# Turning keys and queries one slot later, and queueing the P*V norm ahead of a slot's other evacuations

## The chip, the cores and the metric

One core of one Trainium2 chip. The metric is the device time of one execution in microseconds (us). An execution counts as slow when it is over 1.5% above the fastest of the same kernel, and as fast otherwise. Medians are of all executions of a kernel; ratios use the fast ones alone, and a profile that fell on a slow one is marked. TensorE (PE in the profile; PEld are its weight loads) multiplies matrices, VectorE (DVE) and ScalarE (ACT) empty its results out of PSUM, GpSimd (POOL) converts inputs, SyncE (SP) issues nearly all DMAs.

## The reference

```python
# q, k, v: (8 batches, 8 heads, 576 rows, 64), float32
scores = scale * np.matmul(q, k.transpose(0, 1, 3, 2))
thresh = np.max(scores, axis=-1, keepdims=True) - tau
scores = np.where(scores >= thresh, scores, -1000000000.0)
scores = scores - np.max(scores, axis=-1, keepdims=True)
attn = np.exp(scores)
attn = attn / (np.sum(attn, axis=-1, keepdims=True) + 1e-09)
x = np.matmul(attn, v)        # ... reordered to (8*576, 512)
h = (x @ w1) * (x @ w2) @ w3
return h @ w_out
```

## The kernel before

Two heads of a batch form a "pair" (32 pairs), a pair has nine chunks of 128 score rows, and the kernel is one software-pipelined loop over 288 "slots", one chunk each. The order in which the program calls the operations is the order in each engine's queue. Cut to what matters here:

```python
for t in range(end + 1):
    if t < total:
        scores(t)                  # TensorE: 4 matmuls into a tile S (tag "S", 3 buffers)
    if 0 < t <= total:
        maximum(t - 1)             # VectorE: row maximum and copy; frees that S
    leave()                        # evacuation of the last feed-forward product
    while later: later.pop(0)()    # SyncE: the two DMAs that make kB
    while late: late.pop(0)()      # VectorE: copies of turned keys or queries
    # ... ScalarE's masks and exponentials; DMA transposes of finished probabilities (SyncE)
    if 0 <= c < total and PATH[c % 4] == "P":
        select(c)                  # VectorE: every fourth chunk
    if t in norms:
        next(norms[t])             # VectorE: reciprocal, and x = av * reciprocal; frees av
    if t % 3 == 0 and 0 < t <= total:
        threshold(t - 1)
    # ...
    for f, a in plan.pop(t, ()):
        f(*a)                      # turns, P*V (attend), loads, casts
    # ... then feed-forward matmuls, as TensorE's clock of the plan allows
```

Three kinds of tile share the three score buffers: the scores S, the result `av` of P*V (one per pair, filled at the ends of two consecutive slots) and `tp`, in which TensorE turns the keys or queries of a later pair:

```python
def turn(n, nm):
    tp = psum.tile([128, 2048], BF16, tag="S", name="tp", bufs=3)
    for i, src in enumerate(blocks):                       # 9 transposes on TensorE
        nc.tensor.transpose(tp[:, i * 128:(i + 1) * 128], src, ident[:, :])
    def way():                                             # one slot later
        nc.vector.tensor_copy(st, tp[:, 0:2 * S])          # kT or qT; frees tp
        if nm == "k":
            def swap():                                    # one more slot later
                nc.sync.dma_start(kB[0:64, :], st[64:128, :])
                nc.sync.dma_start(kB[64:128, :], st[0:64, :])
            later.append(swap)
    late.append(way)
```

The scores need kT and kB, the keys with their two halves exchanged. A free buffer goes to the next tile in the order in which the freeing instructions are queued (pair 16 in the prediction shows it).

## Time and profile before

| | before |
|---|---|
| time, median of 3 (range) | 522.89 us (522.27 to 523.69) |
| profiled span | 520.3 us |
| steady state, slots 36 to 252 (24 pairs) | 346.8 us, 14.45 us a pair |
| TensorE busy in it | 93%, VectorE 88%, ScalarE 84% |
| feed-forward products left for the end | 54.8 us |

The steady state is where a change of order can act. TensorE leads in it, so the idle stretches in front of its instructions, by what ended them, are the quantity to follow. The lines are shown in the prediction.

### The profile page before, as it was taken

What the parts mean: (1) busy time and instruction counts of PE and PEld (TensorE: products, weight loads), DVE (VectorE), ACT (ScalarE), POOL (GpSimd) and SP (SyncE); (2) the same over time, 40 slices, a digit from 0 to 9 for tenths busy, and PEclk for the clock granted to TensorE, in tenths of its full rate; (3) what the DMA queues carried; (4) which work ended last, traced back from release to release, by engine and by line L of the source; (5) the groups of instructions that cost most, each with busy time, mean ns of one, the idle gap of its engine ahead of it and who ended that gap; (6) DMA issues with size and microseconds to landing.
All of it is one profiled execution on the core that took longest, in us unless ns stands there. A gap on an engine that the chain in (4) does not pass through costs nothing.

```text
span 520.3 us, 13159 instructions
## 1 busy us (share of the span) xinstructions
PE 471.9 (91%) x4922; PEld 327.0 (63%) x4982; DVE 421.3 (81%) x987; ACT 411.0 (79%) x711; POOL 176.9 (34%) x265
## 2 busy tenths in 40 slices
PE   4788989999999999979998999999988999999996
PEld 3566666666666666656665666666656767554674
DVE  4999988899988898969888988888999988773222
ACT  3798887888889888958898888788878998895442
POOL 6958630443318231543217330631276100000000
PEclk9999999999999999989999999999999999999999
DMA  8999627989899997998799999999999974873211
GB/s 238 197 227 194 159 66 145 182 173 189 171 209 222 196 204 165 218 196 180 152 235 217 192 221 193 204 178 205 208 200 260 214 139 97 151 137 70 82 49 73
DMA packets 203936, 91.15 MB, mean 175 GB/s; under 512 B 169696, under 2 KB 195296, under 8 KB 203872
## 3 DMA queue, kind: packets, MB, share of 16 engines
q1 hardware_dynamic: 199936, 84.54, 77.3%
q0 software_dynamic: 3392, 5.24, 6.0%
q8 instruction: 39, 0.64, 0.5%
q10 hardware_dynamic: 544, 0.52, 0.3%
q14 instruction: 25, 0.20, 0.1%
HBM read 39.32 MB, written 9.44 MB: 94 GB/s over the span
## 4 chain that ended last, share of the span: by engine, by line
PE 54%; DVE 19%; ACT 13%; issue 7%; DMA 6%; SPq 1%; DVEq 0%; ACTq 0%
PE ab L445 14%; PE S L252 13%; PE yp L460 9%; DVE sc L277 7%; ACT y L333 5%; PE av L367 4%; PE both L445 4%; DVE pm L347 3%; DMA pTm<-pms 3%; ACT pm L337 3%; PE tp L203 3%; DVE x L373 3%; PE wp L134 2%; ACT e L343 2%; PE S L258 2%
## 5 line engine op out<-in xcount | busy, mean ns | idle before, releaser
L277 DVE TENSOR_SCALAR_CACHE_REDUCE sc<-S 128x576 f32<-128x576 f32 x288 | 215.0, 751 | 29.7 <-PE S L252 19.6
L333 ACT ACTIVATE y<-sc,thr 128x576 bf16<-128x576 f32 x216 | 162.4, 769 | 11.6 <-DVE thr L285 11.5
L252 PE MATMUL S<-kT,qT 128*128 128x288 bf16 x464 | 125.1, 290 | 12.3 <-DVE x L373 8.9
L252 PE MATMUL S<-kB,qT 128*128 128x288 bf16 x464 | 124.6, 289 | 3.3 <-DMA kB<-kT 3.2
L337 ACT ACTIVATE pm<-y 128x576 bf16<-128x576 bf16 x192 | 126.5, 674 | 0.0
L252 PEld LDWEIGHTS <-qT 128*128 128x128 bf16 x928 | 84.6, 99 | 58.2 <-DVE x L373 12.7
L460 PE MATMUL yp<-wcb,ab 128*128 128x512 bf16 x269 | 67.5, 379 | 1.1 <-ACT ys L452 0.2
L430 DVE TENSOR_TENSOR ab<-ah,ab 128x512 bf16<-128x512 bf16 (+1 forms) x65 | 42.1, 648 | 26.3 <-PE ab L445 22.3
L427 ACT ACTIVATE ah<-ab 128x512 bf16<-128x512 f32 (+1 forms) x65 | 36.7, 564 | 31.0 <-PE ab L445 30.8
L347 DVE SCALAR_TENSOR_TENSOR pm<-sc,thr,e 128x576 bf16<-128x576 f32 x64 | 59.1, 923 | 0.0
L445 PE MATMUL ab<-xm,w1b 128*128 128x512 bf16 x211 | 56.6, 379 | 1.9 <-ACT xm L397 0.9
L445 PE MATMUL ab<-xm,w2b 128*128 128x512 bf16 x203 | 53.7, 379 | 2.1 <-DVE ab L430 0.6
L367 PE MATMUL av<-vb,pT 128*128 128x65 bf16 x1056 | 50.7, 194 | 1.1 <-DMA pT<-pm 1.1
L367 PEld LDWEIGHTS <-pT 128*128 128x128 bf16 x1320 | 47.9, 98 | 4.5 <-DMA pT<-pm 1.3
L445 PEld LDWEIGHTS <-w1b 128*128 128x128 bf16 x352 | 34.1, 98 | 24.4 <-issue 4.5
L343 ACT ACTIVATE e<-sc 128x576 f32<-128x576 f32 x72 | 48.4, 673 | 0.4 <-DVE sc L277 0.4
L445 PEld LDWEIGHTS <-w2b 128*128 128x128 bf16 x352 | 33.6, 98 | 21.2 <-issue 3.1
L452 ACT ACTIVATE ys<-yp 128x512 f32<-128x512 f32 x36 | 21.4, 595 | 30.0 <-PE yp L460 30.0
L460 PEld LDWEIGHTS <-ab 128*128 128x128 bf16 x288 | 27.8, 98 | 25.0 <-issue 0.3
L367 PE MATMUL av<-vz,pT 128*128 128x65 bf16 x256 | 42.6, 192 | 0.0
L161 POOL CAST khl<-kf 128x512 bf16<-128x512 f32 x31 | 20.1, 647 | 58.0 <-DMA kf<-in_k_dram 41.3
L162 POOL TENSOR_TENSOR qhl<-qf,qhl 128x512 bf16<-128x512 f32 x31 | 37.5, 1209 | 2.5
(105 smaller groups left out, 739.8 us busy)
## 6 DMA issues: line engine op xcount, KB each, us to landing
vf<-in_v_dram SPq DMA_DIRECT2D x32, 256.0 KB, 3.4
out_dram<-ys SPq DMA_DIRECT2D x16, 512.0 KB, 3.8
kB<-kT SPq DMA_DIRECT2D x56, 144.0 KB, 3.5
kf<-in_k_dram SPq DMA_DIRECT2D x31, 256.0 KB, 3.7
qf<-in_q_dram SPq DMA_DIRECT2D x31, 256.0 KB, 3.5
w<-in_moe_w_dram POOLq DMA_DIRECT2D x8, 256.0 KB, 5.2
pT<-pm SPq DMA_TRANSPOSE x112, 3.7
kt<-in_k_dram SPq DMA_DIRECT2D x16, 64.0 KB, 3.1
```

What stands on the lines that cost most here:

```text
L162: lo.tensor_tensor(hl[1], src, hl[0], ALU.subtract)
L252: nc.tensor.matmul(sp[:, half, 0:HB], lhsT=t["qT"][:, q0:q0 + 128], rhs=kk[w][:, c0:c0 + HB], start=(w == 0), stop=(w == 1))
L277: nc.vector.tensor_scalar(sc[:, :].rearrange("p (a b) -> p a b", a=2), sp[:, :, 0:HB], 1.0, -3e38, ALU.mult, ALU.max, accum_out=maxima[c / ...
L333: nc.scalar.activation(t["y"][:, :], t.pop("sc")[:, :], AF.Prelu, scale=-1.0, bias=t.pop("thr"), alpha=0.125 / CUT)
L337: nc.scalar.activation(place(*stream[c]), chunks.pop(c)["y"][:, :], AF.Exp, scale=-CUT)
L343: nc.scalar.activation(t["e"][:, :], t["sc"][:, :], AF.Exp, scale=0.125)
L347: nc.vector.scalar_tensor_tensor(out=place(*stream[c]), in0=t["sc"][:, :], scalar=t["thr"], in1=t["e"][:, :], op0=ALU.is_ge, op1=ALU.mult)
L367: nc.tensor.matmul(dst, lhsT=lhsT, rhs=rhs, start=(g == 0), stop=(g == 4))
L427: return lambda: nc.scalar.activation(ah[:, 0:nt], p[:, 0:nt], AF.Copy)
L430: return lambda: nc.vector.tensor_tensor(ab[:, 0:nt], ah[:, 0:nt], p[:, 0:nt], ALU.mult)
L445: nc.tensor.matmul(p[:, 0:nt], lhsT=w[:, c, f * 128:(f + 1) * 128], rhs=x(c), start=(c == 0), stop=(c == 3))
L460: nc.tensor.matmul(yp[0:c1 - c0, :], lhsT=abs_[f][:, c0:c1], rhs=wcb[:, f, :], start=(f == 0), stop=(f == NF - 1))
```

## The change

The norm waits behind whatever VectorE has in its queue in that slot, and TensorE's next scores wait for the norm. The change puts the norm right behind the maximum, and moves the turns so that the key transposes no longer fall into the slot of the norm.

```diff
-    turns = {n: (first[n] - 8, first[n] - 6) for n in range(2, NPAIR)}
+    turns = {n: (first[n] - 7, first[n] - 5) for n in range(2, NPAIR)}
@@
             if 0 < t <= total:
                 maximum(t - 1)
+            if t in norms:
+                next(norms[t])
             leave()
@@
                 select(c)
-            if t in norms:
-                next(norms[t])
             if t % 3 == 0 and 0 < t <= total:
```

Pairs 0 and 1 and the last batch (pairs 28 to 31) keep their turns. The plan counts the conversions on GpSimd and the loads of keys, queries, values and tail rows from the turns, so for the moved pairs these come one slot later too.

## The prediction

> **What bounds the kernel now.** I read the page's busy shares first, then the busy time by stretch, the waits, one pair of heads in order of time, and SyncE's queue. The kernel walks through 288 chunks of scores ("slots"), nine to a pair of heads. From 66.4 to 413.2 us (slots 36 to 252, so 24 pairs of 14.45 us) it is in a steady state, which this row shows; the feed-forward products that are left run alone from 465 us on.
>
> ```profile
> PE 471.9 (91%) x4922; PEld 327.0 (63%) x4982; DVE 421.3 (81%) x987; ACT 411.0 (79%) x711; POOL 176.9 (34%) x265
> ...
> core 0: us, PE busy (x) PEld busy (x) DVE busy (x) ACT busy (x) POOL busy (x), PEclk, DMA share, GB/s
> 66.40:413.20 346.80, 320.86 (x3456) 223.16 (x3499) 305.81 (x717) 291.27 (x505) 128.86 (x166) 1.00 0.94 193
> ```
>
> In the steady state TensorE is busy for 320.86/346.80 = 93%, VectorE for 88%, ScalarE for 84%: three engines close to their limit that wait for each other in turn, with TensorE in front. No instruction is worth much, but an idle stretch of TensorE is. These are TensorE's waits that the change touches, with one of VectorE's:
>
> ```profile
> engine line waited for: us in total, times, longest us
> ...
> DVE ab L430 <- PE ab L445: 22.3, 26, 5.0
> ...
> PEld L252 <- DVE x L373: 12.7, 21, 1.2
> ...
> PE S L252 <- DVE x L373: 8.9, 18, 1.0
> ...
> PEld L252 <- DMA kB<-kT: 4.3, 4, 2.1
> ...
> PE S L252 <- DMA kB<-kT: 3.2, 3, 1.9
> ```
>
> The largest steady wait of TensorE is the score matmuls' wait for the norm x (8.9 us in 18 pairs, about 0.85 us in every second pair and 0.2 to 0.33 in the others). The PEld row is the same wait seen by the weight loads, not another 12.7 us. The second wait is for kB, the copy of the keys with its halves exchanged by DMA. Here is the norm's wait in pair 16:
>
> ```profile
> start us, us, engine line op out<-in xcount [idle before <-releaser]
> ...
> 239.58 0.74 DVE L277 TENSOR_SCALAR_CACHE_REDUCE sc<-S 128x576 f32<-128x576 f32 x1
> ...
> 241.03 0.69 DVE L430 TENSOR_TENSOR ab<-ah,ab 128x512 bf16<-128x512 bf16 x1 [0.69 <-PE ab L445]
> ...
> 241.25 0.39 PE L203 MATMUL tp<-ident,khl 128*128 128x128 bf16 x4
> ...
> 241.63 0.21 DVE L371 RECIPROCAL rcp<-av 128x10 f32<-128x10 f32 x1
> ...
> 241.88 0.82 DVE L373 TENSOR_TENSOR x<-av,rcp 128x640 bf16<-128x640 f32 x1
> ...
> 242.76 0.30 PE L252 MATMUL S<-kT,qT 128*128 128x288 bf16 x1 [0.85 <-DVE x L373]
> ```
>
> What to see: P*V (av) was finished at 240.05, and VectorE's maximum of the slot with its read-out at 240.34. VectorE then sat idle for 0.69 us until TensorE had made the feed-forward product, because that evacuation stands ahead of the norm in its queue. Meanwhile the transposes of the keys (tp) took the score buffer that the maximum had just freed, so the next scores got the buffer of av, which only the norm frees, and TensorE stood for 0.85 us. It is a loop: TensorE's product, its evacuation, the norm, TensorE's scores. I call the slot in which this happens slot 1 of the nine (P*V is made at the ends of slots 8 and 0).
>
> **What the Trainium skill says.** "PSUM — Partial Sum Buffer", section "Engine vs sequencer instructions": the queues of VectorE and ScalarE are strict FIFO. The trace agrees: the norm's inputs lay ready for 1.3 us behind an instruction that itself waited. "Perfetto Trace Analysis", section "Optimization Strategy": the same gap repeating on the engine that should be saturated can mean that there is no SBUF or PSUM left for the next tile. The trace agrees: the gap is a wait for one of three score buffers. The same page, "Identifying the Most-Contended Engine", warns that matmul busy time is no measure of closeness to the limit; here the weight loads are busy for 64% of the stretch against 93% for matmuls, so TensorE can be asked for more than its 7% of idle time suggests. The same page, "DMA Instruction — HWDGE (DVE, Sync)": the issuing sequencer is free only when it has issued, and the data's movement is not in that window. The trace agrees: a kB issue takes about 0.5 us and lands 3.5 us (median) after its start.
>
> **The change, part by part.** No instruction is added, removed or resized: only order changes.
>
> *The norm first.* In slot 1 the norm (0.21 + 0.82 us) moves ahead of the feed-forward evacuation (0.65 us) and of a select (0.92 us, where there is one). By the rows above it would start at 240.34 and end near 241.4 instead of 242.70, and the evacuation, whose product is ready at about 240.9, follows with no idle time.
>
> *The turns one slot later.* The key transposes move from the end of slot 1 to the end of slot 2, the query ones from slot 3 to slot 4. Buffers are handed out in the order in which their readers are queued (pair 16 shows it). So the scores of slot 2 now get the buffer that the maximum of slot 1 frees, and the transposes get av's buffer, one block of scores later. In pair 16: the scores come at 241.3, or at 242.1 if a feed-forward step slips in before them; both are after 240.34, so nothing waits. The transposes come near 242.6, and the norm ended near 241.4: nothing waits. The scores of slot 3 need the maximum of slot 2, which VectorE reaches at 241.4 + 0.7 = 242.1 and ends at 242.9: in time. The whole wait goes, and VectorE's idle 0.69 us is used. Gain: all 18 waits, **-8.9 us**.
>
> *What lateness costs.* kT comes one slot (about 1.55 us) later, and so does its exchange kB, which the scores of the next pair need. SyncE's queue for kB of pair 17:
>
> ```profile
> 244.08 0.47 SPq L226 DMA_DIRECT2D kB<-kT  x1
> 244.60 0.59 SPq L227 DMA_DIRECT2D kB<-kT  x1
> 245.52 2.18 SPq L323 DMA_TRANSPOSE pT<-pm  x1
> 247.79 1.28 SPq L328 DMA_TRANSPOSE pTm<-pms  x1
> ```
>
> kB is queued at the start of slot 3 now, of slot 4 then. The transposed probabilities of slot 3 will stand ahead of it instead of behind: one DMA transpose in pairs n with n mod 4 = 0 or 3, two where n mod 4 = 1, none newly where n mod 4 = 2 (there it is ahead already). I took from the trace, for pairs 6 to 27, when kB landed and when its scores began. The margin is now 4.9 to 5.6 us for the pairs with n mod 4 = 1, 1.9 to 5.4 for 0, -2.1 to 5.2 for 3, -0.9 to 2.5 for 2; three pairs are below zero (15, 18, 26: the three kB waits above). Moving each issue behind those transposes at their old times costs 2.5 to 4.7 us where one is added and 4.1 to 5.0 us where two are. That leaves pairs 17 and 23 at about -0.1, 12 at -0.4, 24 at -0.9, 19 at -2.2, 15 at -4.8, and adds 6.4 us of waiting. If the transposes move up by the 1.2 us of the two kB issues that no longer precede them, wherever their inputs are ready, only pairs 15 and 19 lose more than 0.2 us: 2.6 us in all. I take **+4.5 us**. (Queries have 5.1 us or more to spare and keep 3.5.)
>
> *Small terms.* Pairs 28 to 31 keep their turns, so the queries of pair 27 and the keys of pair 28 fall into one slot, with two copies of 0.75 us: I estimate **+0.5 us**. Thresholds of slot 3 now stand behind the key copy of 0.75 us; ScalarE waits for thresholds 11.5 us in all, but has over 2 us of idle time a pair: 0.
>
> Sum: -8.9 + 4.5 + 0.5 = -3.9 us, from 522.9 to **519.0 us** (-0.7%).
>
> **The rivals.** *A: kB takes the place of the norm.* For it: margins already below zero in three pairs, a DMA share of 0.94 in the steady state, and SyncE's single queue. If the delays are the upper ones, and those pairs push the landings of later ones, the loss is 8 to 12 us and the time 522 to 526. Against it: 10 of the 22 pairs had over 3 us to spare. *B: VectorE takes over.* Its work between two maxima does not shrink, so the scores might wait one block later for the next maximum. For it: 88% busy. Against it: 41 us of idle time in the steady state (346.80 - 305.81), and the gap in slot 1 (idle 0.69 us) that the norm fills. If B held half the gain back: about 523. *C: the loop gains more than its wait.* A shorter cycle also feeds VectorE and ScalarE sooner (VectorE waits 22.3 us for the feed-forward products), and kB's issues have room: 509 to 513. Against it: with the wait gone, a pair such as 16 leaves TensorE no visible idle time at all. *D: the norm waits for P*V.* Queued so early, it may reach VectorE before av is done and block what is behind it. In pair 16 it would not (240.05 against 240.34); where VectorE follows closely it could be 0.1 to 0.3 us a pair, below VectorE's idle time.
>
> **Range and chances.** 519.0 is the sum. From 511.5 (C in part, kB without loss) to 526 (A with part of B) should hold 8 times in 10. Over 2% faster needs less than 512.4, more than the whole wait on the norm: 0.08. Over 2% slower needs 533.3, some 19 us of new waits: 0.02. Within 2%: 0.90.
>
> **What would show it right or wrong.** The rows for TensorE waiting on x should fall from 8.9 us to under 2. The feed-forward evacuation should follow the norm in slot 1 without idle time. The kB waits (3.2 us in 3) should grow to some 6 to 10 us in 4 to 8 pairs, first in pairs 15 and 19; if they stay at 3, the time falls towards 514, and if they pass 12, I was wrong about the sign. A new row of TensorE waiting for sc or for ab in the score matmuls would speak for B. The last stretch of feed-forward products (55 us) should not change. If the time moves by more than 8 us either way while x's wait goes as foreseen, the step on kB is at fault.

## The result, and the profile after

The changed kernel takes 518.09 us (median of 4, 514.77 to 518.31) against 522.96 us of the kernel before in the same rounds. The ratio is 0.9892, with a 95% interval of 0.985 to 0.9934. It is 0.9875 (0.983 to 0.9919) when measured once more below. A ratio is the mean time of one kernel's fast runs over that of the other's of the same rounds, so not quite the ratio of the medians.

The profiled execution of the changed kernel was its fastest, so its span of 513.0 us flatters it by some 3 us. First the busy shares and the steady state (columns as in the prediction's row):

```profile
PE 467.4 (91%) x4922; PEld 325.7 (63%) x4982; DVE 425.2 (83%) x987; ACT 410.4 (80%) x711; POOL 177.9 (35%) x265
...
67.00:405.50 338.50, 316.72 (x3457) 222.07 (x3500) 308.21 (x717) 290.45 (x505) 127.82 (x166) 1.00 0.97 198
```

The same 24 pairs take 338.5 us against 346.8 (14.10 us a pair against 14.45). The last stretch is the same 54.8 us. So the whole gain of this profile lies in the steady state (8.3 us, against 7.3 us of the span). The waits of TensorE in the changed kernel:

```profile
PEld L252 <- DMA kB<-kT: 10.9, 8, 3.0
PE S L252 <- DMA kB<-kT: 9.6, 8, 2.8
...
PEld L367 <- DMA pTm<-pms: 1.5, 2, 1.1
PEld L252 <- DVE x L373: 1.5, 2, 1.0
...
PE av L367 <- DMA pTm<-pms: 1.3, 2, 0.9
...
PE S L252 <- DVE x L373: 1.0, 2, 0.7
```

The wait for x went from 8.9 us in 18 places to 1.0 in 2. The wait for kB went from 3.2 us in 3 places to 9.6 in 8. P*V's wait for the DMA-transposed probabilities (pT and pTm) fell from 4.2 us (3.1 + 1.1) to 1.7 (1.3 + 0.4).

Pair 16 shows how the wait for x went. This is the same slot 1 as in the prediction's lines:

```profile
234.76 0.76 DVE L277 TENSOR_SCALAR_CACHE_REDUCE sc<-S 128x576 f32<-128x576 f32 x1 [0.30 <-ACT pm L337]
...
235.46 0.22 DVE L371 RECIPROCAL rcp<-av 128x10 f32<-128x10 f32 x1
...
235.72 0.82 DVE L373 TENSOR_TENSOR x<-av,rcp 128x640 bf16<-128x640 f32 x1
...
236.46 0.68 DVE L430 TENSOR_TENSOR ab<-ah,ab 128x512 bf16<-128x512 bf16 x1
...
237.48 0.29 PE L252 MATMUL S<-kT,qT 128*128 128x288 bf16 x1
...
237.97 0.39 PE L203 MATMUL tp<-ident,khl 128*128 128x128 bf16 x4
```

The norm follows the maximum at once, the feed-forward evacuation follows the norm with no idle time in brackets, and the scores of slot 2 and then the key transposes start with no wait. SyncE's queue for kB of pair 17, whose counterpart stands in the prediction:

```profile
240.11 1.28 SPq L323 DMA_TRANSPOSE pT<-pm  x1
241.48 1.24 SPq L328 DMA_TRANSPOSE pTm<-pms  x1
242.81 0.54 SPq L226 DMA_DIRECT2D kB<-kT  x1
243.40 0.59 SPq L227 DMA_DIRECT2D kB<-kT  x1
```

kB now stands behind two transposes. In this pair it landed 1.7 us before its scores began. Before the change it had 4.9 us to spare.

### The profile page after: what moved, and what is told of

It reads as the page before. It is cut to its first block, busy times and chain, and to the rows that moved or that the text cites.

```text
span 513.0 us, 13187 instructions
## 1 busy us (share of the span) xinstructions
PE 467.4 (91%) x4922; PEld 325.7 (63%) x4982; DVE 425.2 (83%) x987; ACT 410.4 (80%) x711; POOL 177.9 (35%) x265
## 2 busy tenths in 40 slices
DMA packets 203936, 91.15 MB, mean 178 GB/s; under 512 B 169696, under 2 KB 195296, under 8 KB 203872
## 4 chain that ended last, share of the span: by engine, by line
PE 61%; DVE 14%; DMA 8%; ACT 7%; issue 6%; POOL 3%; SPq 0%; DVEq 0%; ACTq 0%; POOLq 0%
PE S L252 15%; PE ab L445 14%; PE yp L460 10%; PE av L367 6%; DVE sc L277 6%; PE tp L203 4%; PE both L445 4%; DMA kB<-kT 3%; PE wp L134 3%; ACT y L333 2%; DVE pm L347 2%; DMA qt<-in_q_dram 2%; PE S L258 2%; DMA pTm<-pms 2%; DVE ab L430 1%
## 5 line engine op out<-in xcount | busy, mean ns | idle before, releaser
L252 PEld LDWEIGHTS <-qT 128*128 128x128 bf16 x928 | 86.0, 98 | 55.5 <-DMA kB<-kT 10.9
L347 DVE SCALAR_TENSOR_TENSOR pm<-sc,thr,e 128x576 bf16<-128x576 f32 x64 | 55.3, 864 | 0.0
L162 POOL TENSOR_TENSOR khl<-kf,khl 128x512 bf16<-128x512 f32 x31 | 36.6, 1181 | 2.5
```

What stands on the lines that cost most here:

```text
L162: lo.tensor_tensor(hl[1], src, hl[0], ALU.subtract)
L252: nc.tensor.matmul(sp[:, half, 0:HB], lhsT=t["qT"][:, q0:q0 + 128], rhs=kk[w][:, c0:c0 + HB], start=(w == 0), stop=(w == 1))
L347: nc.vector.scalar_tensor_tensor(out=place(*stream[c]), in0=t["sc"][:, :], scalar=t["thr"], in1=t["e"][:, :], op0=ALU.is_ge, op1=ALU.mult)
```

## The experiments

Twelve kernels ran, all correct except two. Every one was timed in 5 rounds against the kernel before, and one profile was taken of each. The kernels of one group ran on one chip and share the runs of the kernel before (medians 524.49, 526.82, 526.38 and 524.71 us in the four groups). Ratios are against the kernel before.

### First group: which part of the change does it?

**The changed kernel again.** No edit.

> The changed kernel once more, for common rounds and a second profile, since its profiled execution (514.8 us) was 3.3 us below its three others (518). Theory 1 (the gain is the wait on the norm minus new waits for kB): ratio 0.986 to 0.993, waits of the score matmuls on x under 2 us, on kB 8 to 11 us in about 8 places. Rival (the fast profile was the rule and part of the gain is something else): ratio under 0.985.

Ratio 0.9875 (518.87 us median, 514.59 us the fastest). In its profile x costs 1.0 us and kB 12.1 us in 7 places. 4.0 us of that is one wait for pair 1's kB at the very start, where 0.6 us stood in the first profile and 0.1 us in the kernel before. Its steady state is 338.1 us, as in the first profile. The two profiles differ by 4.9 us, and the start makes 5.3 us of it (slot 36 is reached at 72.3 us against 67.0). So the fast first profile was luck at the start, and the gain of 8 us in the steady state repeats. Part of it is lost at the start, though: by the profiles, kernels with the old turns reach slot 36 at 66.4 to 67.8 us, and those with late turns (leaving out kB on ScalarE) at 66.5 to 72.3. Half-clock stretches before slot 36 (3.4 to 6.8 us) occur only among the latter. Why the start suffers is not shown. kB's 12.1 us lie above the 8 to 11 expected; without pair 1 they are 8.1.

**The turns alone.** The norm goes back to its old place.

```diff
-            if t in norms:
-                next(norms[t])        # ahead of leave()
+            if t in norms:
+                next(norms[t])        # behind select(c), as before
```

> The turns one slot later, the norm at its old place. Theory 1: the scores of slot 2 no longer get av's buffer, so their wait on x goes also without the early norm; the key transposes now wait for the norm instead, 0.1 to 0.7 us in every second pair, 3 us in all; kB as in the changed kernel, 8 to 11 us. Ratio 0.990 to 0.999. Rival (the early norm carries the gain): the wait on x moves whole to the transposes, 8 us or more, and the ratio is 1.00 to 1.01.

Ratio 0.988 (0.9839 to 0.9921): the same as the whole change. The waits in its profile:

```profile
PE S L252 <- DMA kB<-kT: 6.3, 6, 1.8
...
PE av L367 <- DMA pTm<-pms: 1.7, 2, 1.4
...
PE tp L203 <- DVE x L373: 1.4, 2, 1.0
```

The scores' wait for x fell to 0.3 us in one place, and 1.4 us of waiting for x turned up at the key transposes instead (3 us were expected). So the later turns alone remove the wait, as they should if the scores of slot 2 take the buffer that a maximum frees. The ratio is better than the 0.990 to 0.999 expected, and kB costs 6.3 us where 8 to 11 were expected. The early norm on top of it is worth nothing that these runs can show.

**The norm alone.** The turns go back to their old slots.

```diff
-    turns = {n: (first[n] - 7, first[n] - 5) for n in range(2, NPAIR)}
+    turns = {n: (first[n] - 8, first[n] - 6) for n in range(2, NPAIR)}
```

> The norm first, the turns at their old slots: kB is as early as before. Theory 1: the norm ends near 1.8 us after the slot's maximum began, before TensorE reaches the scores of slot 2, so the wait on x falls from 8.9 to 0 to 3 us while kB waits stay at 3 to 4 us: ratio 0.980 to 0.988, faster than the changed kernel by 2 to 5 us. Rival (without the other buffer the scores still meet the norm): 4 us or more of the wait on x stay, ratio 0.990 to 1.000.

Ratio 0.9986 (0.9937 to 1.0036): nothing gained that these runs can show, against 0.980 to 0.988 expected. The theory failed here; the ratio lies where the rival put it, but not for the rival's reason, which needed 4 us or more of waiting for x. Its profile:

```profile
PE av L367 <- DMA pTm<-pms: 6.0, 4, 2.8
PEld L252 <- DVE x L373: 5.6, 13, 1.0
PE S L252 <- DMA kB<-kT: 5.2, 4, 2.8
...
PE S L252 <- DVE x L373: 3.1, 12, 0.7
```

The wait for x did fall, by 5.8 us, to within a tenth of the upper end of what was expected. But the waits for pT, pTm and kB together rose from 7.4 us to 12.4 (6.0 + 1.2 + 5.2), and TensorE's clock was halved for 6.8 us and for 3.4 us in the loop, against 3.4 us once in the kernel before. The timed executions say the same: their mean granted clock is 0.988, against 0.9935 for the kernel before in the same rounds. SyncE's queue has the same order as in the kernel before, so a new order in it is not what made these DMAs late. Why they were late is not shown. The waits for pT and pTm differ much between profiles with the old turns: 4.2 us in the kernel before, 7.2 here, and 7.6 (6.6 + 1.0) in the kernel with the old turns and pair 1's kB made on TensorE (third group).

**kB into SyncE's queue at once.** The changed kernel, but the DMAs are queued in the slot of the key copy, ahead of that slot's transposes.

```diff
-                later.append(swap)
+                swap()
```

> The changed kernel, with the exchange of the keys put into SyncE's queue in the slot of the key copy, ahead of that slot's transposes, not at the start of the next slot. Theory 1: kB is issued within 0.3 us of the end of the key copy in most pairs, its waits fall from about 9.6 to 2 to 5 us, and the kernel gains 3 to 6 us on the changed one: ratio 0.976 to 0.984. Rival (kB's lateness costs nothing on the whole, since TensorE, once ahead, would wait for something else): kB waits fall but the time stays within 1.5 us of the changed kernel's, with longer waits for transposed probabilities or maxima.

Ratio 0.9981: worse than the changed kernel by about 1%, where a gain was expected. kB was issued within 0.05 us of the end of the key copy in seven of the pairs 6 to 27 (in none of them in the changed kernel), not in most of them as expected, and its waits are 7.7 us in 3 places, against 9.6 to 12.1 in the changed kernel and 2 to 5 expected. But pT and pTm rose from 1.7 us to 5.9 (3.0 + 2.9), and the clock was halved three times within the loop, each time around a single wait of 3.0 to 3.4 us. In this profile the transposes lose in SyncE's queue what kB gains, and the few waits that are left are long enough to halve the clock.

### Second group: what is kB worth?

**kB from ScalarE's queue.** `nc.scalar.dma_start` in place of `nc.sync.dma_start` in `swap`.

> The changed kernel with the two kB exchanges issued from ScalarE's queue instead of SyncE's. Theory 2 (SyncE's single queue is a second bound: whichever of kB and the transposed probabilities is put first, the other comes late): kB waits fall under 4 us and those for transposed probabilities stay under 2.5 us, ratio to the kernel before 0.973 to 0.983. Rival (the DMA engines themselves, busy 0.97 of the time, are the bound): kB still lands late, waits stay at 7 us or more, ratio 0.985 to 0.992; or ScalarE pays for issuing, with the same ratio.

Ratio 0.9972. It doesn't settle the question it was made for. kB waits did fall to 3.8 us in one place (pair 1), but ScalarE itself then stood for 11.1 us behind the issue of pair 2's kB, and slot 36 was reached at 79.3 us against 67.0. The steady state was 340.9 us, not better than the changed kernel's. The clock was halved for 13.7 us before slot 36 and twice for 3.4 us after it, and the profile fell on the slowest of the six executions. The ratio lies outside what either the theory (0.973 to 0.983) or its rival (0.985 to 0.992) had said.

**No kB, in the changed kernel and in the kernel before.** The scores read kT where they read kB. The results are wrong, the engines' work is the same; 56 DMAs and their places in SyncE's queue go with kB.

```diff
+                t["kB"] = st
+                return
                 def swap():
```

> The changed kernel without the exchange: the scores read kT where they read kB (wrong result on purpose, same work on the engines, 56 DMAs fewer). Sizes what waiting for kB costs the changed kernel. Prediction's step (6.4 us more of kB waits): waits of 9 to 12 us go, ratio 0.968 to 0.978. Rival (what kB no longer takes, transposed probabilities take): ratio 0.980 or more with waits for pT and pTm of 5 us or more.

> The kernel before, without the exchange (wrong result on purpose). Only 3 us of kB waits can go: ratio 0.990 to 0.998. Against b2 it gives what the change is worth when kB cannot be late: theory 2 says 9 to 11 us (the waits on x of 8.9 us and part of the key transposes' waits for maxima of 2.2 us). Rival: the difference stays at 5 to 6 us, and kB had no part in it.

The ratios are 0.9661 and 0.9777. Two things follow. First, kB with its DMAs costs far more than the 3.2 us that the row of waits shows: without it the kernel before gains 2.2%, 11.8 us at the means of the fast runs (515.05 against 526.82 us), where 1 to 5 us were expected. In its profile the waits for kB (3.2 us) are gone and those for pT and pTm fell from 4.2 to under 2 us. Most of the rest can be clock: the mean granted clock of its runs is 0.9994 against 0.9902, which over 520 us is 4.8 us of TensorE's time (an estimate). Second, the change is worth 0.9661/0.9777 = 0.988 without kB, the same as with it. The rival's number was right here: the gain was expected to grow to 9 to 11 us, and stayed at 6 us. By the two profiles it is 8.5 us in the steady state (330.6 against 339.1), as with kB, and slot 36 comes 3.1 us later (70.3 against 67.2).

The rows of waits say what fills the place:

```profile
PE tp L203 <- DVE sc L279: 2.6, 4, 1.2
PE S L254 <- DVE sc L279: 2.0, 4, 0.8
...
PE tp L203 <- DVE x L375: 1.5, 4, 0.4
```

These are the changed kernel's without kB. In the kernel before without it, the scores wait longest for x:

```profile
PE S L254 <- DVE x L375: 8.5, 19, 0.9
```

In the changed one this row is 1.0 us. So x falls by 7.5 us, and TensorE waits for VectorE a little more elsewhere: scores for a maximum 2.2 us with line 260 (before 1.3) and transposes for x 1.5 us (before 0.2). Lines 254, 260, 279 and 375 are lines 252, 258, 277 and 373, moved by the edit.

**The turns one slot later still.**

```diff
-    turns = {n: (first[n] - 7, first[n] - 5) for n in range(2, NPAIR)}
+    turns = {n: (first[n] - 6, first[n] - 4) for n in range(2, NPAIR)}
```

> The changed kernel with the turns one further slot later. The wait on x stays away. Prediction's step (each kB is later by the time of the transposes that get ahead of it, and margins are used up): kB comes 1.5 us or more later against margins of 0 to 2 us, so its waits grow to 18 to 30 us and the ratio to 0.998 to 1.03. Rival (lateness of kB is given and taken within SyncE's queue): kB waits under 14 us, ratio under 0.993.

Ratio 1.0013 (0.9976 to 1.0051): the whole gain is gone. kB costs 21.0 us in 13 places, within the 18 to 30 us expected, and x still 1.0 us.

```profile
PE S L252 <- DMA kB<-kT: 21.0, 13, 3.8
```

Lateness of kB is therefore not given and taken within SyncE's queue: past its margin it is paid. In this kernel the clock was halved four times in the loop, each time at such a wait (1.98 to 3.85 us). One of them, first in order of time on TensorE, then by stretch (busy us of the engines, then granted clock, DMA share and GB/s):

```profile
268.96 0.28 PE L252 MATMUL S<-kT,qT 128*128 128x288 bf16 x1
271.43 0.42 PE L252 MATMUL S<-kB,qT 128*128 128x288 bf16 x1 [2.19 <-DMA kB<-kT]
271.65 0.45 PE L252 MATMUL S<-kT,qT 128*128 128x288 bf16 x1
```

```profile
265.00:271.40 6.40, 4.19 (x51) 2.70 (x49) 4.55 (x13) 5.73 (x10) 1.07 (x2) 1.00 0.93 191
271.40:274.90 3.50, 3.25 (x31) 2.37 (x33) 1.88 (x5) 0.00 (x0) 0.00 (x0) 0.52 1.05 269
274.90:281.00 6.10, 6.10 (x52) 4.09 (x50) 5.48 (x13) 4.92 (x10) 1.14 (x3) 1.00 1.19 182
```

After 2.19 us of waiting the same matmul takes 0.45 us in place of 0.29, and for 3.4 us the granted clock is a half.

The Trainium skill, page "TensorE: Matmul & The Clock Gate", section "What's actually happening", says that the clock falls to a half after at least one idle window of about 3.4 us, and that the window runs freely. The traces agree on the window: up to 470 us every halved stretch lasts 3.4 or 6.8 us and starts on a fixed grid of 3.41 us, counted from the first full-speed record of its trace. They don't agree on idle: in the 3.4 us before this stretch TensorE's matmuls were busy for 1.24 us. In all 14 profiles up to 470 us (slow ones included), each of the 21 grid windows at full clock whose matmuls were busy for at most 0.44 of it was followed by a halved one, none of the 1797 above 0.525 was, and 2 of the 13 between were.

So each long wait can cost itself and up to 1.7 us more for every 3.4 us at half clock (half of it, an estimate), and whether it does depends on how it falls on the grid. A wait of 2.81 us in the changed kernel had no such stretch: it lay across two windows, busy for 2.05 and 1.89 of 3.4 us. Nor had one of 2.85 us in the kernel with the norm alone (2.14 and 1.76).

### Third and fourth group: the start, and the tail loads

**Pair 1's kB on TensorE**, in the changed kernel and in the kernel before, as a remedy for the wait at the start.

```diff
-        tp2 = psum.tile(...) if n == 0 and nm == "k" else None
+        tp2 = psum.tile(...) if n < 2 and nm == "k" else None
```

> The changed kernel, with the exchanged keys of pair 1 made by a second set of transposes on TensorE and a copy on ScalarE (as pair 0 already does) instead of by DMA. Theory: the wait for pair 1's kB (0.6 us in one profile of the changed kernel, 4.0 us in another, followed by 6.8 us at half clock) makes most of the spread between executions; without it the ratio is 0.978 to 0.986 and the spread halves. Rival (the extra transposes and copy cost as much): ratio 0.987 or more.

> The kernel before with pair 1's exchanged keys made on TensorE. Control for c1: the same start, the old turns. Theory: ratio 0.992 to 1.000, waits on x at 8 to 9 us; c1 against this gives the change without the chance of the start: 6 to 9 us. Rival (the late turns also lengthen the start of the kernel): 5 us or less.

The ratios are 0.996 (0.9906 to 1.0013) and 0.9989 (0.9951 to 1.0028). The remedy missed. The spread did not halve: the fast runs of the first lie between 518.71 and 525.94 us. Its granted clock is 0.987, against 0.9953 for the second, so it ran longer at half clock, though this edit lies at the start only. (Its profile fell on an execution counted as slow.) Here the change gained only about 0.3% (1.5 us), where 6 to 9 us were expected. Why is not shown. A guess: the changed kernel sits close to an edge, and with margins of kB near zero at several pairs a shift at the start can turn short waits into long ones. The rival of the second kernel (5 us or less, because the late turns lengthen the start) fits the number. The distance from the 0.988 found twice is little more than the noise of these ratios.

**Tail loads from GpSimd's queue.** The six DMAs that load the tail rows of a new batch stand in SyncE's queue shortly before the late kBs. They move to another queue (the first batch's keep theirs), first together with the last edit.

```diff
-    def load_tail(b, nm, queue=nc.sync):
+    def load_tail(b, nm, queue=nc.gpsimd):
```

> As c1, and the loads of the tail rows of each batch (six DMAs within two pairs) issued from GpSimd's queue instead of SyncE's. Theory 2 (SyncE's queue is what makes kB late at the batch boundaries, pairs with n mod 4 = 2 and 3): kB waits fall from about 9 us to under 5 us, ratio 0.968 to 0.978. Rival (the DMA engines, busy 0.97 of the time, or the transposes before kB make it late): kB waits stay at 8 us or more and the ratio within 0.003 of c1.

The ratio is 0.9794 (0.9745 to 0.9843; 513.70 us), a little above the 0.968 to 0.978 expected, against 0.996 in the same rounds without this edit. In its profile only two kB waits are left, and the wait for x is as in the changed kernel:

```profile
PE S L252 <- DMA kB<-kT: 3.0, 2, 2.3
...
PE av L367 <- DMA pTm<-pms: 1.7, 2, 1.4
...
PE S L252 <- DVE x L373: 1.0, 2, 0.7
```

No clock was halved before the end, and the steady state is 334.5 us. Then the same edit on the changed kernel itself, pair 1 as it was:

> The changed kernel with the tail rows of batches 1 to 7 loaded from GpSimd's queue, pair 1 as in the changed kernel: the step from c1 to c2 alone, on the changed kernel itself. Theory 2 (six issues of 0.65 us each stand ahead of kB in SyncE's queue at every batch boundary): kB waits of 3 to 6 us with pair 1's chance wait, ratio 0.974 to 0.983. Rival (the gap between c1 and c2 was chance in how the DMAs fell): kB waits of 8 us or more, ratio 0.986 or more.

Ratio 0.9711 (0.9663 to 0.9758), 511.69 us as the median of seven executions of which two count as slow, the fastest at 507.8: better than expected, and faster than both kernels of this study. (Its profile fell on an execution counted as slow, with 6.9 us of kB waits where 3 to 6 were expected; the waits are read from the kernel above.) The two slow executions are left out of the ratio, but their lower clock (0.989 and 0.993) may be half-clock stretches like those above: with all executions of both kernels it is 0.975.

The traces show where the gain comes from. In the twelve pairs of 6 to 27 with n mod 4 = 2 or 3, near the batch boundaries, kB was issued 4.1 us after the end of the key copy in the changed kernel (mean), and 1.9 us after it with pair 1's kB on TensorE and the tail loads moved; in the other ten pairs 3.3 us in both. From issue to landing it took no less (3.8 and 4.1 us in the twelve). So SyncE's queue at the batch boundaries was a large part of what made kB late, although the DMA engines' share was 0.97. The bytes are the same (91.15 MB), but the DMA packets are not: 203,936 before the tail loads moved and 192,176 after. Whether that helped too is not tested.

## Why the prediction was right or wrong

The time was foreseen: 519.0 us against 518.09 and 518.87 measured, a gain of 1.1 to 1.25% against 0.7%. How near it came is in part luck. The steady state gained 8.3 and 8.6 us in the two profiles, twice the predicted sum of 3.9 us, and the start, which the prediction left out, took back 0.6 and 5.9 us of it.

*The norm's wait goes: -8.9 us.* It went: 8.9 to 1.0 us. The mechanism was right for pair 16, step by step. Two things can be held against it. First the size: the prediction called the weight loads' row (12.7 us) the same wait and took the matmuls' row. A matmul's modelled end lies later than the moment at which the next could have started (score matmuls of 0.29 us start 0.12 us apart in pair 16), so the matmuls' row is the smaller one. On the weight loads' rows the accounts of the first profile come near: x -11.2 (12.7 to 1.5), kB +6.6 (4.3 to 10.9), pTm and pT -3.2 (5.2 to 2.0), together -7.8 us, where the profiled span fell by 7.3. In the second profile the same rows give -5.3 us where the span fell by 2.4, so neither row is a rule; time at half clock is in none of them. Second the credit: it gave the two parts a joint effect. The turns alone give all of it (0.988), the norm alone none (0.9986).

*kB's lateness: +4.5 us, between 2.6 and 6.4.* The matmuls' waits for kB grew by 6.4 us in the first profile and by 8.9 us in the second (of which 3.9 us are pair 1, whose turn did not change). The upper estimate was nearer. Pair 17's place behind two transposes came as foreseen. In the first profile the worst margins are those of pairs 26 (-3.1 us), 15 and 19 (-1.8 each), 11 (-1.3) and 24 (-1.1): pairs 15, 19 and 24 were named, 11 was not, and 15 was taken for -4.8 us. Turning one slot later still confirmed that lateness is paid. The mark "if they pass 12, I was wrong about the sign" was too strict: the second profile has 12.1 us, and the gain repeated. That the loss by kB takes back half of the gain is not what the runs without kB show: there the change is worth the same 6 us, and by the rows, waits for VectorE's maxima and for x (rival B in small) grow when kB doesn't hold TensorE back. One reading was wrong without consequence: 5.2 us, given as the highest margin for n mod 4 = 3, is pair 3's; among pairs 6 to 27 it is 3.9 us.

*Terms that were missing.* P*V's waits for transposed probabilities fell by 2.5 us. That fits kB no longer standing ahead of their transposes: these waits are 4.2 to 7.6 us in the four kernels where it does (the one before, the norm alone, kB at once, and the old turns with pair 1's kB on TensorE) and 0.4 to 2.2 us in the others with their kB in SyncE's queue, or none. But with kB on ScalarE they are 6.3 us, so the cause is not shown. The prediction used that to reduce kB's delay, but did not count it as a gain. And a long wait can cost more than itself, by the halved clock.

*The small terms.* Nothing in the last stretch changed, as foreseen. The collision of pairs 27 and 28 cannot be told from the rest: the stretch from slot 252 to 287 took 52.7 us against 52.3.

*The rivals.* A (kB in place of the norm) is real, at about the size given, and is what sets the next limit, as the tail loads show. B is small here: the scores' waits for a maximum (lines 252 and 258) went from 1.8 to 2.2 us. C (more than the wait) can't be excluded for the steady state, which gained 8.3 us in the profile, one halved stretch of the kernel before included. D was not seen in pair 16.

What stays open is why the norm alone gains nothing although its wait for x falls by 5.8 us. Long DMA waits take its place in the profile and in the granted clock of its runs, but their cause is not shown.

## What to carry to other kernels

When an engine waits for a buffer, ask first which buffer the next tile gets and who frees it. Moving the tile that takes the wrong one brought the wait from 8.9 to 0.3 us here and the time down with it; moving the freeing instruction up brought the wait to 3.1 us and the time nowhere that these runs can show. When work is moved later, list what stands ahead of its DMA in the queue that issues it, and give a queue that is full at a known place (here the batch boundary) fewer DMAs: moving six loads per batch to another queue was worth more than the change itself.

## What the Trainium skill lacked or had wrong

- "TensorE: Matmul & The Clock Gate", section "HAM oscillation — how this bites in real kernels", gives the rule as no idle gaps over about 3.4 us. Here waits of 1.98 and 2.19 us went with 3.4 us at half clock, and waits of 2.81 and 2.85 us did not. What told them apart was the busy share of TensorE's matmuls in one window of the 3.41 us grid: up to 0.44 the next window was halved (21 of 21), above 0.525 never (0 of 1797). The page gives no such share.
- "Perfetto Trace Analysis", section "Tensor Engine Instruction (MATMUL, LD_WEIGHTS)", says that a matmul's end is an estimate, but not which row to take for lost time. For the same stops the matmuls' row here shows 8.9 us and the weight loads' row 12.7. The sum of the latter's changes was near the change of the span in one profile (-7.8 and -7.3 us) and not in the other (-5.3 and -2.4).
- "DMA: Bandwidth & Descriptors", section "Issuing engines are not separate DMA queues", says that issuing DMAs from several engines only saves the sequencer's time for issuing, "which is usually small relative to the DMA itself". In this case it is not small: in the changed kernel's steady state a DMA transpose holds SyncE's queue for 1.2 to 3.4 us (median 1.3), against 3.1 us from a kB's issue to its landing (median), and kB stands behind it. Moving six loads per batch to another queue, with the same bytes, brought the ratio to the kernel before from 0.9875 to 0.9711.
